# Gate and up of the later chunks with 76 products per tile pair instead of 78

## The chip, the cores and the metric

One core of a Trainium2 chip runs the whole program. The metric is the device time of one execution in microseconds; of several runs the median is taken. TensorE is written PE here, its weight loads PEld, VectorE DVE, ScalarE ACT, GpSimd POOL and SyncE, which issues the transfers, SP.

## What is computed

The reference normalizes 8192 tokens of 448 channels, mixes them with a spectral layer (a Fourier transform over the tokens, a small block MLP on each frequency, the inverse transform), adds the result to the input, normalizes again and adds a gated feed-forward layer:

```python
h = _layernorm(x) * (1 + ca) + sa
x = x + ga * _A_ref(h, A_w1, A_b1, A_w2, A_b2)           # rfft2, block MLP, shrink, irfft2
h = _layernorm(x) * (1 + cb) + sb
x = x + gb * ((_gelu(h @ w_gate) * (h @ w_up)) @ w_down)  # 448 -> 1792 -> 448
```

The change lies in the last line alone: the products `h @ w_gate` and `h @ w_up` of most tokens, and what prepares their operands.

## The kernel before

The spectral part fills the first 360 us. Then the tokens pass in 32 chunks of 256 (two blocks of 128). Every float32 operand of the feed-forward layer is held as two fp16 parts, hi and lo, and a product is the sum of hi by hi, hi by lo and lo by hi.

**Chunks 0 to 7** (`NSTD = 8`) compute gate and up in the plain way: `gate_up(i, k)` for k = 0 to 13 in the matmuls of line 1240, each followed by GELU (1276) and a multiplication (1281), by sums on GpSimd (`sums`, 1289 to 1292) and by a cut of the result into hi and lo (`quantize`, 1300 and 1301).

**Chunks 8 to 31** use a scheme in the manner of Strassen and Winograd. Channels and hidden units are split in two, the tokens of a chunk too, and seven products (A11, S1, S2, A12, S4, A22, S3, each with its own form of the weights and of the tokens) replace eight. A unit of work is one tile pair: 128 hidden units of each half, for gate and up (`pr` = 0 and 1). `mm(u, reg, f, x)` issues one of the seven; its list `terms` names the hi and lo parts, and each entry is one matmul for gate and one for up. 448 channels make 224 to a half, which is one tile of 128 rows and one of 96. The second tile is packed: the last 64 channels (384 to 448) are handled so that both halves of a tile's rows carry something. A11, S1 and S2 take five entries, the other four six, together 39 entries or 78 matmuls to a unit, in line 1483. Seven units (`NP = 7`) make a chunk, 24 chunks make 168 units.

A period of that stage issues `stage_a` of unit u, `stage_d` of u - 2, `stage_c` of u - 1 and `stage_b` of u on PE; between them stand ScalarE's copies of PSUM (`copy_b`, 1511, and `seed`, 1515), VectorE's sums (`joins`, 1520 and 1526), GELU (1532, 1540) and the multiplications (1536, 1543). Once a chunk the down projection of the chunk before runs between them (`phase`, `down`).

**Operands of the later chunks.** The token forms of chunk i + 1 or i + 2 are packed into the tile `pk` (25 tiles of 128 columns): ScalarE writes the hi parts (`wpack_hi`, line 1454), GpSimd the lo parts (`wpack_lo`, 1460), in five pieces k. Two such tiles alternate. SyncE transposes them in five transfers of five tiles into `nt` (`wtransposes`, 1466). The weight forms are made once, **during chunks 1 to 7**, for one tile t a chunk: `load_forms` loads raw weights `wr`, `form_sums` adds and subtracts their quarters a11, a12, a21, a22 on GpSimd (1673 to 1677), `forms_hi` and `forms_lo` cut each form n into hi on ScalarE (1707) and lo on VectorE (1712), and `store_forms` writes them to DRAM (1721). Form S2 = a21 + a22 - a11 has a tile of its own, `wf`.

**What sets the order.** Each engine works through its instructions in the order in which the code issues them. The tables `start` and `steady` name the place of each step of the preparation: a number is the index k of `gate_up` behind which it stands, and `m0`, `m1`, `m2` are three places inside `down`. In chunks 2 to 7 it is `steady` that holds. The splits of g and v for the inverse transform of a later chunk (`split_g`, `split_v`, line 117) are issued behind k = 1, the preparation of k = 2 after them.

`down(i, banks, mid)` runs seven products of 21 matmuls (lines 1313 to 1315). In chunks 0 to 7 it takes two banks of PSUM in turn for all products but the second. Its middle is

```python
S.copy(p1, product(i, heads[0][1], 0, rest))
V.tensor_tensor(o11, product(i, heads[1][1], 1, rest), p1, ALU.add)
mid(0)
S.copy(p4, product(i, banks(2), 2))
mid(1)
V.tensor_tensor(u2, product(i, banks(3), 4), p1, ALU.add)
V.tensor_tensor(u4, product(i, banks(4), 3), u2, ALU.add)
mid(2)
```

`S.copy(p1, ...)` is line 1340, `S.copy(p4, ...)` 1346, the sum u2 1349, the sum u4 1350. The product with `banks(4)` uses the bank that the copy p4 empties.

Of the kernel before, what the change touches and what calls it, by code (L numbers as in the profile page):

```python
# [10 lines left out]
F32 = mybir.dt.float32  # L11
F32R = mybir.dt.float32r
F16 = mybir.dt.float16
# [3 lines left out]
ALU = mybir.AluOpType  # L17

N = 8192
D = 448  # L20
# [4 lines left out]
CB = 2  # L25
# [10 lines left out]
PKW = 2 * D + 64  # L36
PKO = [0, 128, 256, 384, 448, 576, 704, 832]
NTT = len(PKO)
NXT = 25
LA = 2  # L40
NSTD = 8
WPARTS = ((0, 4), (4, 7))
# [8 lines left out]
def spectral_geglu(ctx, tc, x, w1, b1, w2, b2, wg, wu, wd, cvec, wmod, cf1, cs2, cmi, cgm, out):  # L51
    nc = tc.nc
    V, S, G, T = nc.vector, nc.scalar, nc.gpsimd, nc.tensor
# [90 lines left out]
    with ExitStack() as actx:  # L144
# [26 lines left out]
        q, y, t, nm, mu = (ap.tile([128, NB], F32, name=nm) for nm in ("q", "y", "t", "nm", "mu"))  # L171
# [201 lines left out]
        for g, bs in enumerate(groups):  # L373
            e = bs[-1]
# [34 lines left out]
    with ExitStack() as bctx:  # L409
# [225 lines left out]
        side = {}  # L635
# [87 lines left out]
        n = NB // 4  # L723
# [25 lines left out]
        raws = {}  # L749
# [208 lines left out]
        for n, i in enumerate([3, 4, 5, 5, 6, 7, 7, 8, 9, 10, 11, 12, 13, 14]):  # L958
            j, pr = divmod(n, 2)
# [26 lines left out]
        draws, nxt, x1t = {}, {}, {}  # L986

        x1s, x1n = [ep.tile([128, CB, D], F32, name="x10")], {}
# [6 lines left out]
        cp = None  # L995
# [96 lines left out]
    with ExitStack() as cctx:  # L1092
        cp = cctx.enter_context(tc.tile_pool(name="cp", bufs=1, side="right"))
        H = 128 * CB
        pkt = cp.tile([128, NXT * 128], F16, name="pk")
        wds = wds + [cp.tile([128, 2, 7, HC], F16, name=f"wd{t}") for t in range(len(wds), NP)]
        x1s += [cp.tile([128, CB, D], F32, name=f"x1{n}") for n in (1, 2)]
        pkts = [pkt]
        nts, acts, pgu, outs = {}, {}, {}, []

        def nt_tile():
# [330 lines left out]
        def pk_of(i):  # L1432
            return pkts[max(0, i - NSTD) % 2]

        def pieces(i, k):

            n, p = nxt[i]["n"], pk_of(i)
            if k == 0:
                return [(n[:, 0, 0:192], p[:, 0:192], [(128, 192, p[:, 192:256]), (0, 128, p[:, 256:384])])]
            if k in (1, 2):  # L1440
                o = (1152, 1664)[k - 1]
                return [(n[:, k - 1, 192:448], p[:, o : o + 256], [(0, 256, p[:, o + 256 : o + 512])])]
            if k == 3:
                p = p[:, 384:1152].rearrange("p (j c) -> p j c", j=2)
                src = nxt[i]["t"][:, 0:384].rearrange("p (j c) -> p j c", j=2)
                return [(src, p[:, :, 0:192], [(128, 192, p[:, :, 192:256]), (0, 128, p[:, :, 256:384])])]
            p = p[:, 2176:3200].rearrange("p (j c) -> p j c", j=2)
            src = nxt[i]["t"][:, 384:896].rearrange("p (j c) -> p j c", j=2)
            return [(src, p[:, :, 0:256], [(0, 256, p[:, :, 256:512])])]

        def wpack_hi(i, ks):
            for k in ks:
                for src, hi, _ in pieces(i, k):
                    S.copy(hi, src)

        def wpack_lo(i, ks, e=G):
            for k in ks:
                for src, hi, los in pieces(i, k):
                    for a, b, lo in los:
                        e.tensor_tensor(lo, src[..., a:b], hi[..., a:b], ALU.subtract)  # L1460

        def wtransposes(i, gs, w=5):
            if i not in nts:
                nts[i] = nt_tile()
            for g in gs:
                nc.sync.dma_start(
                    nts[i][:, w * g : w * g + w, :], pk_of(i)[:, 128 * w * g : 128 * w * (g + 1)], transpose=True
                )

        A11, S1, S2, A12, S4, A22, S3 = range(7)  # L1470
        B11, T1, T2, B21, B22, T3, T4 = 0, 3, 6, 9, 13, 17, 21
        RV, RY, RX = 0, 1, 2

        def mm(u, reg, f, x, start=False):

            ps2, slot, nt = sets[u % 3], wslot[slot_of[u]], nts[u // NP]
            if f in (A11, S1, S2):
                terms = [(0, f, x), (0, f, x + 2), (1, f, x), (0, 7 + f, x + 1), (1, 7 + f, x + 1)]
            else:
                terms = [(l, f + 7 * g, x + g + 2 * m) for g in range(2) for l, m in ((0, 0), (0, 1), (1, 0))]  # L1480
            for j, (hl, wt, xt) in enumerate(terms):
                for pr in range(2):
                    T.matmul(  # L1483
                        ps2[:, pr, reg * 128 : reg * 128 + 128],
                        slot[:, pr, hl, wt, :],
                        nt[:, xt, :],
                        start=start and j == 0,
                        stop=j == len(terms) - 1,
                        skip_group_check=True,
                    )  # L1490
# [175 lines left out]
        def form_sums(t, part):  # L1666
            r = raws[("w", t)]
            a11, a12, a21, a22 = (r[:, q, h : h + 3].rearrange("p c x -> p (c x)") for q in range(2) for h in (0, 3))
            if part == 0:
                raws[("f", t)] = cp2.tile([128, 384], F32, tag="wf", name="wf")  # L1670
            s2 = raws[("f", t)]
            if part == 0:
                G.tensor_tensor(a21, a21, a22, ALU.add)
                G.tensor_tensor(s2, a21, a11, ALU.subtract)
            else:
                G.tensor_tensor(a12, a12, s2, ALU.subtract)
                G.tensor_tensor(s2, a22, s2, ALU.subtract)

        def form_cut(t, n):

            w, r, s2 = raws[("s", t, n // 5)], raws[("w", t)], raws[("f", t)].rearrange("p (c x) -> p c x", c=3)
            tq = r[:, :, 6:7]
            f, c, src = [
                (A12, 0, r[:, 0, 3:6]),
                (A12, 3, tq[:, 0]),
                (A11, 0, r[:, 0, 0:3]),
                (S1, 0, r[:, 1, 0:3]),
                (S2, 0, s2),
                (A22, 0, r[:, 1, 3:6]),
                (S4, 3, tq[:, 0]),  # L1690
                (A22, 3, tq[:, 1].to_broadcast([128, 2, 128])),
                (S4, 0, r[:, 0, 3:6]),
                (S3, 0, s2),
            ][n]
            f0 = WPARTS[n // 5][0]

            def out(l):
                return w[:, l, 0:3, f - f0] if c == 0 else w[:, l, 3, f - f0 : f - f0 + src.shape[1]]

            return out(0), out(1), src  # L1700

        def forms_hi(t, *ns):
            for n in ns:
                if n % 5 == 0:
                    raws[("s", t, n // 5)] = cp2.tile([128, 2, 4, 4 - n // 5, 128], F16, tag=f"ws{n}", name="ws")
                hi, _, src = form_cut(t, n)
                S.activation(hi, src, AF.Copy, scale=sww)

        def forms_lo(t, *ns):
            for n in ns:  # L1710
                hi, lo, src = form_cut(t, n)
                V.scalar_tensor_tensor(lo, src, sww, hi, op0=ALU.mult, op1=ALU.subtract)
                if n == 4:
                    w = raws[("s", t, 0)]
                    V.tensor_copy(w[:, :, 3, 0:3], w[:, :, 2, 0:3])

        def store_forms(t, part):
            w = raws.pop(("s", t, part))
# [8 lines left out]
            ("m1", forms_lo, 0),  # L1727
            ("m1", forms_hi, 2),
            ("m2", forms_lo, 2),
            ("m2", forms_hi, 1, 3),  # L1730
            (3, forms_lo, 1, 3),
            (3, forms_hi, 4),
            (4, forms_lo, 4),
            (4, form_sums, 1),
            (4, forms_hi, 5),
            (5, forms_lo, 5),
            (5, forms_hi, 6, 7),
            (5, store_forms, 0),
            (6, forms_lo, 6, 7),
            (6, forms_hi, 8),  # L1740
            (7, forms_lo, 8),
            (7, forms_hi, 9),
            (8, forms_lo, 9),
            (9, store_forms, 1),
        ]
        steady = [
# [15 lines left out]
            (3, forms_lo, 6, 7),  # L1762
            (4, forms_hi, 8),
            (5, forms_lo, 8),
            (5, forms_hi, 9),
            (6, forms_lo, 9),
            (7, store_forms, 1),
        ]
        prep = {}
# [83 lines left out]
        pack_lo(0)  # L1853
        down_lo(0, range(1, 2))
        fctx.close()
        cp2 = cctx2.enter_context(tc.tile_pool(name="cp2", bufs=1))
        load_d8(2)
        load_g(1)
# [70 lines left out]
        pkts.append(cp2.tile([128, NXT * 128], F16, name="pk2"))  # L1929
        x1s.append(cp2.tile([128, CB, D], F32, name="x13"))  # L1930

        opening = {
# [13 lines left out]
        for u in range(U0, NT_ + 1):  # L1946
            period(u)
            i, k = divmod(u, NP)
# [99 lines left out]
```

## Time and profile before

| | us |
|---|---|
| median of three runs | 1865.55 |
| lowest and highest | 1863.15, 1866.06 |
| the profiled execution | 1862.79 |
| its span, first to last instruction | 1861.0 |
| line 1483: 13104 matmuls, in union | 736.5 |
| lines 1313 to 1315 into `pdn`: each 1218 matmuls, in union | 315 to 316 |
| line 1240: 2464 matmuls, in union | 268.3 |

A group's time is the union of its instructions, and matmuls overlap (each lasts longer than the distance to the next), so the groups' times don't add up to PE's. A row of the timeline gives the start, the length, the engine, the line, the operation, output and input, and in brackets how long the engine stood idle before it and what ended that.

### The profile page before, as it was taken

To read this page: it belongs to the slowest core of one execution; us is meant where nothing else is said; L and a number is where in the kernel's file an instruction comes from. 1 tells how busy PE (TensorE), PEld (TensorE's weight loads), DVE (VectorE), ACT (ScalarE), POOL (GpSimd) and SP (SyncE) were. 2 spreads that over 40 slices of the span, in tenths; PEclk is the share of its full clock that TensorE was granted. 3 is DMA by queue.
4 is the path that set the end of the run, shared out by engine and by line. 5 is a ranking of instruction groups with operands and counts; after the bars stand their busy time and mean duration, and the time that the engine had idled before them with its cause. 6 is when DMAs were issued, how large, how long until landed. Compare 5 with 4: busy or idle time off the path is not lost.

```text
span 1861.0 us, 56443 instructions
## 1 busy us (share of the span) xinstructions
PE 1821.3 (98%) x23376; PEld 1726.6 (93%) x23376; DVE 1410.8 (76%) x2895; ACT 973.6 (52%) x1828; POOL 1313.2 (71%) x1705
## 2 busy tenths in 40 slices
PE   7999999899999999999999999999999999999998
PEld 3698999788888899999999999999999999999998
DVE  8787999878766677777777777777777777777755
ACT  5776778544444444555555555555554444444443
POOL 3476878258777778777777777777777777777544
PEclk9999999999999999999999999999999999999999
DMA  9987778744444446966766666666666676666551
GB/s 355 337 288 250 234 202 230 206 106 104 105 104 104 104 105 171 248 170 171 171 176 177 174 176 172 171 172 174 178 173 178 173 175 175 174 176 174 154 158 55
DMA packets 380089, 330.48 MB, mean 178 GB/s; under 512 B 110260, under 2 KB 358200, under 8 KB 379832
## 3 DMA queue, kind: packets, MB, share of 16 engines
q1 hardware_dynamic: 379832, 326.87, 64.0%
q8 instruction: 183, 3.00, 0.7%
q14 instruction: 74, 0.61, 0.1%
HBM read 243.32 MB, written 60.10 MB: 163 GB/s over the span
## 4 chain that ended last, share of the span: by engine, by line
PE 86%; DVE 6%; DMA 3%; ACT 2%; SPq 1%; POOL 1%; issue 1%; ACTq 0%; DVEq 0%
PE set L1483 39%; PE pgu L1240 11%; PE pdn L1313 6%; PE pdn L1315 6%; PE pdn L1314 6%; PE ps L213 2%; PE set L1315 2%; PE set L1314 2%; PE set L1313 2%; DVE y L556 1%; DVE hl L486 1%; PE set L1607 1%; PE pm L539 1%; PE ps L451 1%; DVE st L174 1%
## 5 line engine op out<-in xcount | busy, mean ns | idle before, releaser
L1483 PE MATMUL set<-nt,wk 128*128 128x128 f16 x13104 | 736.5, 219 | 3.1 <-ACT sb L1511 1.6
L1483 PEld LDWEIGHTS <-wk 128*128 128x128 f16 x13104 | 733.9, 98 | 3.5 <-issue 2.4
L1315 PE MATMUL pdn<-wd,ac 128*128 128x224 f16 x1218 | 315.5, 259 | 0.6 <-DVE ac L1301 0.6
L1313 PE MATMUL pdn<-wd,ac 128*128 128x224 f16 x1218 | 315.7, 259 | 0.0
L1314 PE MATMUL pdn<-wd,ac 128*128 128x224 f16 x1218 | 315.5, 259 | 0.0
L1240 PE MATMUL pgu<-nt,wk 128*128 128x256 f16 (+1 forms) x2464 | 268.3, 273 | 3.8 <-DVE x L1281 3.8
L1240 PEld LDWEIGHTS <-wk 128*128 128x128 f16 (+1 forms) x2464 | 225.8, 98 | 44.9 <-issue 19.3
L1532 ACT ACTIVATE gl<-c,dg 128x384 f32<-128x384 f32 x168 | 103.5, 616 | 229.9 <-DVE c L1526 227.0
L1558 DVE SCALAR_TENSOR_TENSOR ac<-x,sa_act,ac 128x896 f16<-128x896 f32 x168 | 205.9, 1226 | 19.9 <-ACT ac L1548 19.8
L1289 POOL TENSOR_TENSOR x<-x 128x128 f32<-128x128 f32 x223 | 129.8, 582 | 119.9 <-DVE x L1281 58.5
L1359 POOL TENSOR_TENSOR cq<-cq 128x224 f32<-128x224 f32 x32 | 21.1, 660 | 261.8 <-DVE cq L1358 261.8
L1290 POOL TENSOR_TENSOR x<-x 128x128 f32<-128x128 f32 x223 | 186.3, 836 | 17.5
L1548 ACT ACTIVATE ac<-x,sa_act 128x896 f16<-128x896 f32 x168 | 174.2, 1037 | 13.8 <-POOL x L1292 6.6
L1536 DVE TENSOR_TENSOR x<-c,gl 128x384 f32<-128x384 f32 x168 | 154.3, 918 | 17.3 <-ACT gl L1532 17.0
L1313 PEld LDWEIGHTS <-ac 128*128 128x128 f16 x1568 | 153.4, 98 | 4.9 <-issue 4.8
L1315 PEld LDWEIGHTS <-ac 128*128 128x128 f16 x1568 | 153.4, 98 | 0.8 <-DVE ac L1301 0.8
L1314 PEld LDWEIGHTS <-ac 128*128 128x128 f16 x1568 | 153.5, 98 | 0.1
L1520 DVE TENSOR_TENSOR c<-set,sb 128x512 f32<-128x512 f32 x168 | 115.3, 687 | 35.6 <-PE set L1483 35.6
L1276 ACT ACTIVATE gel<-pgu,dg 128x256 f32<-128x256 f32 x112 | 49.5, 471 | 157.9 <-PE pgu L1240 150.3
L1291 POOL TENSOR_TENSOR x<-x 128x128 f32<-128x128 f32 x223 | 131.8, 591 | 0.0
L1511 ACT COPY sb<-set 128x512 f32<-128x512 f32 x168 | 97.6, 581 | 62.0 <-PE set L1483 60.7
L117 POOL TENSOR_TENSOR yl<-y,yh 128x448 fp32r<-128x448 f32 x63 | 87.9, 1413 | 54.9 <-ACT yh L115 54.6
(334 smaller groups left out, 3837.1 us busy)
## 6 DMA issues: line engine op xcount, KB each, us to landing
wk<-wk SPq DMA_DIRECT2D x76, 1024.0 KB, 8.9
wk<-wk SPq DMA_DIRECT2D x76, 768.0 KB, 5.7
tr<-td SPq DMA_DIRECT2D x32, 448.0 KB, 4.9
vd<-us SPq DMA_DIRECT2D x64, 224.0 KB, 3.1
xx<-in_A_x SPq DMA_DIRECT2D x32, 448.0 KB, 4.5
v<-vd SPq DMA_DIRECT2D x63, 224.0 KB, 5.5
out<-x SPq DMA_DIRECT2D x31, 448.0 KB, 7.0
xt<-in_A_x SPq DMA_DIRECT2D x15, 896.0 KB, 14.7
```

Source lines behind the costliest of these rows:

```text
L1240: T.matmul(pgu[i, t, q][:, pr * H : (pr + 1) * H], ws[rows, n, w, tw], nts[i][rows, tn, :], start=start, stop=stop, skip_group_check=True,)
L1289: e.tensor_tensor(s1, a21, a22, ALU.add)
L1290: e.tensor_tensor(s2, s1, a11, ALU.subtract)
L1291: e.tensor_tensor(s3, a11, a21, ALU.subtract)
L1313: T.matmul(ps, ac[:, 0, ka], w[:, 0, kb], start=n == 0, stop=False)
L1314: T.matmul(ps, ac[:, 0, ka], w[:, 1, kb], start=False, stop=False)
L1315: T.matmul(ps, ac[:, 1, ka], w[:, 0, kb], start=False, stop=n == NP - 1)
L1483: T.matmul(ps2[:, pr, reg * 128 : reg * 128 + 128], slot[:, pr, hl, wt, :], nt[:, xt, :], start=start and j == 0, stop=j == len(terms) - 1 ...
L1520: V.tensor_tensor(c[:, :, 1:3, :], p[:, :, 0:256].rearrange("p g (r c) -> p g r c", r=2), b[:, :, 0:128].rearrange("p g (o c) -> p g o c", ...
L1536: V.tensor_tensor(xs[u][:, 1::3, :], cts.pop(u)[:, 1], gls.pop(u), ALU.mult)
L1548: S.activation(ac[:, 0], xs[u][:, 0:7], AF.Copy, scale=sa_act[:, t : t + 1])
L1558: V.scalar_tensor_tensor(ac[:, 1], xs.pop(u)[:, 0:7], sa_act[:, t : t + 1], ac[:, 0], op0=ALU.mult, op1=ALU.subtract)
```

## The change

It takes one of the six entries from S4, which makes 76 matmuls to a unit, and lets half-used tiles of A11, S2 and S4 carry the terms of the last 64 channels. For that,

- the weight forms hold other things in their packed halves: `form_sums` makes a difference of the last 64 channels' weights (`e1`), form 7 of before goes, form S3 gets a packed column of its own, and small copies and one addition (`forms_lo`, `forms_hi`) fill the halves;
- `form_sums` has three parts instead of two, and the tile `wf` goes: S2 overwrites a11, which it may do once `forms_hi` and `forms_lo` of form 2 (A11) have read a11. So it moves from place 0 to place 2 in `steady`;
- the packed tokens have 27 tiles instead of 25: 7 in `pkx`, of which there are two, and 20 in `pk`, of which there is one. The first transpose takes seven tiles, the other four take five;
- one of the buffers for x moves to another pool.

The core of the diff:

```diff
 def wpack_hi(i, ks):
+    n = nxt[i]["n"]
     for k in ks:
         for src, hi, _ in pieces(i, k):
             S.copy(hi, src)
+        if k == 2:
+            for src, o in ((n[:, 1, 320:384], 1152), (n[:, 0, 128:192], 1280), (n[:, 1, 384:448], 2496)):
+                S.copy(pkt[:, o : o + 64], src)
+        if k == 3:
+            S.copy(pkt[:, 2432:2496], nxt[i]["t"][:, 320:384])
...
+            if k == 2:
...
+                e.tensor_tensor(rest, a, b, ALU.subtract)
+                el = pkx_of(i)[:, 832:896]
+                e.tensor_tensor(el, el, rest[:, 1], ALU.subtract)
...
-    if f in (A11, S1, S2):
-        terms = [(0, f, x), (0, f, x + 2), (1, f, x), (0, 7 + f, x + 1), (1, 7 + f, x + 1)]
+    if f in (A11, S1, S2, S4):
+        x4, x5 = {A11: (x + 1, TA), S1: (x + 1, x + 1), S2: (x + 1, TY), S4: (x + 3, x + 1)}[f]
+        terms = [(0, f, x), (0, f, x + 2), (1, f, x), (0, 7 + f, x4), (1, 7 + f, x5)]
...
 def form_sums(t, part):
...
     if part == 0:
         G.tensor_tensor(a21, a21, a22, ALU.add)
-        G.tensor_tensor(s2, a21, a11, ALU.subtract)
+    elif part == 1:
+        G.tensor_tensor(a11, a21, a11, ALU.subtract)
     else:
-        G.tensor_tensor(a12, a12, s2, ALU.subtract)
-        G.tensor_tensor(s2, a22, s2, ALU.subtract)
+        e1, e2 = r[:, 0, 6], r[:, 1, 6]
+        G.tensor_tensor(e1, e2, e1, ALU.subtract)
+        G.tensor_tensor(a12, a12, a11, ALU.subtract)
+        G.tensor_tensor(a11, a22, a11, ALU.subtract)
...
 steady = [
...
     (2, forms_lo, 2),
+    (2, form_sums, 1),
     (2, forms_hi, 1),
     ("m0", forms_lo, 1),
     ("m0", forms_hi, 3, 4),
...
     ("m2", forms_lo, 4, 5),
-    ("m2", form_sums, 1),
-    ("m2", forms_hi, 6, 7),
+    ("m2", form_sums, 2),
+    ("m2", forms_hi, 6),
```

How the instructions stand on GpSimd in chunk 2, at the second `gate_up` and the down projection (`x` are the sums, `gl` and `v` the splits, `wr` the quarters of the weights, `wf` S2; 1359 belongs to the down projection). Before:

```order
L1673 TENSOR_TENSOR wr<-wr 128x384
L1674 TENSOR_TENSOR wf<-wr 128x384
L1289 TENSOR_TENSOR x_7216<-x_7216 128x128
L1290 TENSOR_TENSOR x_7216<-x_7216 128x128
L1291 TENSOR_TENSOR x_7216<-x_7216 128x128
L1292 TENSOR_TENSOR x_7216<-x_7216 128x128
L117 TENSOR_TENSOR gl<-g,gh 128x256
L117 TENSOR_TENSOR v<-v,vh 128x896
L1676 TENSOR_TENSOR wr<-wr,wf 128x384
L1677 TENSOR_TENSOR wf<-wr,wf 128x384
L1359 TENSOR_TENSOR cq_3433<-cq_3432 128x224
```

With the change:

```order
L1683 TENSOR_TENSOR wr<-wr 128x384
L1289 TENSOR_TENSOR x_7221<-x_7221 128x128
L1290 TENSOR_TENSOR x_7221<-x_7221 128x128
L1291 TENSOR_TENSOR x_7221<-x_7221 128x128
L1292 TENSOR_TENSOR x_7221<-x_7221 128x128
L117 TENSOR_TENSOR gl<-g,gh 128x256
L117 TENSOR_TENSOR v<-v,vh 128x896
L1685 TENSOR_TENSOR wr<-wr 128x384
L1688 TENSOR_TENSOR wr<-wr 128x128
L1689 TENSOR_TENSOR wr<-wr 128x384
L1690 TENSOR_TENSOR wr<-wr 128x384
L1359 TENSOR_TENSOR cq_3433<-cq_3432 128x224
```

S2 (1674 before, 1685 now) moved from ahead of the four sums and the two splits to behind them.

ScalarE in the down projection of the same chunk (1340 is the copy p1, 1346 the copy p4, the two rows between them are the hi parts of forms S1 and S2). Before:

```order
L1707 ACTIVATE ws<-wr,sww 128x128
L1340 COPY cq_3432<-pdn 128x224
L1707 ACTIVATE ws<-wr,sww 128x3x128
L1707 ACTIVATE ws<-wf,sww 128x3x128
L1346 COPY cq_3432<-pdn 128x224
```

With the change:

```order
L1719 ACTIVATE ws<-wr,sww 128x128
L1340 COPY cq_3432<-pdn 128x224
L1719 ACTIVATE ws<-wr,sww 128x3x128 x2
L1346 COPY cq_3432<-pdn 128x224
L1719 ACTIVATE ws<-wr,sww 128x3x128
```

Nothing moved here: the hi part of S2 stands ahead of the copy p4 in both, and reads `wf` before and `wr` (a11) now.

GpSimd in chunk 7, where the tokens of chunk 8 are packed as well. Before:

```order
L1426 COPY x_10642<-n_10542 128x64
L1460 TENSOR_TENSOR pk<-n_10542,pk 128x64
L1460 TENSOR_TENSOR pk<-n_10542,pk 128x128
L1460 TENSOR_TENSOR pk<-n_10542,pk 128x256 x2
L1289 TENSOR_TENSOR x_10635<-x_10635 128x128
```

With the change:

```order
L1426 COPY x_10662<-n_10564 128x64
L1467 TENSOR_TENSOR pkx_5786<-n_10564,pkx_5786 128x64
L1467 TENSOR_TENSOR pkx_5786<-n_10564,pkx_5786 128x128
L1467 TENSOR_TENSOR pkx_5786<-n_10564,pkx_5786 128x256
L1467 TENSOR_TENSOR pk<-n_10564,pk 128x128
L1471 TENSOR_TENSOR pk<-n_10564,pk 128x2x64
L1473 TENSOR_TENSOR pkx_5786<-pkx_5786,pk 128x64
L1289 TENSOR_TENSOR x_10657<-x_10657 128x128
```

One subtraction of 256 columns became one of 128, one of two times 64 and one of 64.

More of the change, by code (lines that the diff above doesn't have):

```diff
@@ L38 @@
 NTT = len(PKO)
-NXT = 25
+NXT, NXP = 27, 7
 LA = 2
@@ L1094, in spectral_geglu @@
         H = 128 * CB
-        pkt = cp.tile([128, NXT * 128], F16, name="pk")
+        pkt = cp.tile([128, (NXT - NXP) * 128], F16, name="pk")
+        pkx = [cp.tile([128, NXP * 128], F16, name="pkx0")]
         wds = wds + [cp.tile([128, 2, 7, HC], F16, name=f"wd{t}") for t in range(len(wds), NP)]
-        x1s += [cp.tile([128, CB, D], F32, name=f"x1{n}") for n in (1, 2)]
-        pkts = [pkt]
+        x1s.append(cp.tile([128, CB, D], F32, name="x11"))
         nts, acts, pgu, outs = {}, {}, {}, []
@@ L1460, in wpack_lo, with wtransposes @@
                         e.tensor_tensor(lo, src[..., a:b], hi[..., a:b], ALU.subtract)
-        def wtransposes(i, gs, w=5):
+                    if k == 2:
+                        rest = pkt[:, 1152:1408].rearrange("p (j c) -> p j c", j=2)[:, :, 64:128]
+                        a, b = (v[:, 128:256].rearrange("p (j c) -> p j c", j=2) for v in (src, hi))
+                        e.tensor_tensor(rest, a, b, ALU.subtract)
+                        el = pkx_of(i)[:, 832:896]
+                        e.tensor_tensor(el, el, rest[:, 1], ALU.subtract)
+        def wtransposes(i, gs):
             if i not in nts:
@@ L1465, in wtransposes @@
             for g in gs:
[L1466 to L1471, printed above, removed]
+                t, w, src = (0, NXP, pkx_of(i)) if g == 0 else (NXP + 5 * g - 5, 5, pkt[:, 640 * g - 640 : 640 * g])
+                nc.sync.dma_start(nts[i][:, t : t + w, :], src, transpose=True)
+        A11, S1, S2, A12, S4, S3, A22 = range(7)
+        B11, B21, T1, T2, B22, TA, T3, T4, TY = 0, 3, 7, 10, 13, 17, 18, 22, 26
         RV, RY, RX = 0, 1, 2
@@ L1707, in forms_hi @@
                 S.activation(hi, src, AF.Copy, scale=sww)
+                if n == 7:
+                    w = raws[("s", t, 1)]
+                    S.copy(w[:, 0, 3, 0], w[:, 0, 2, 0])
         def forms_lo(t, *ns):
@@ L1712, in forms_lo @@
                 V.scalar_tensor_tensor(lo, src, sww, hi, op0=ALU.mult, op1=ALU.subtract)
-                if n == 4:
-                    w = raws[("s", t, 0)]
-                    V.tensor_copy(w[:, :, 3, 0:3], w[:, :, 2, 0:3])
+                w, e = raws[("s", t, n // 5)], raws[("s", t, 0)][:, :, 3, 3]
+                if n == 1:
+                    V.tensor_copy(w[:, 1, 3, 0:3:2], e[:, 0:1].to_broadcast([128, 2, 128]))
+                elif n == 4:
+                    V.tensor_copy(w[:, 0, 3, 0:3], w[:, 0, 2, 0:3])
+                    V.tensor_copy(w[:, 1, 3, 1], w[:, 1, 2, 1])
+                elif n == 5:
+                    V.tensor_copy(w[:, 1, 3, 0], e[:, 1])
+                elif n == 6:
+                    V.tensor_tensor(w[:, 1, 3, 1], w[:, 1, 3, 1], w[:, 1, 3, 0], ALU.add)
         def store_forms(t, part):
-            w = raws.pop(("s", t, part))
+            w = raws[("s", t, part)]
             for pr, rows in enumerate(rows2):
@@ L1733, in spectral_geglu @@
             (4, forms_lo, 4),
-            (4, form_sums, 1),
+            (4, form_sums, 2),
             (4, forms_hi, 5),
             (5, forms_lo, 5),
-            (5, forms_hi, 6, 7),
+            (5, forms_hi, 6),
             (5, store_forms, 0),
[L1739 to L1743, printed above, removed]
+            (6, forms_lo, 6),
+            (6, forms_hi, 7),
+            (7, forms_lo, 7),
+            (7, forms_hi, 8),
+            (8, forms_lo, 8),
             (9, store_forms, 1),
@@ L1758, in spectral_geglu @@
             ("m2", forms_lo, 4, 5),
-            ("m2", form_sums, 1),
-            ("m2", forms_hi, 6, 7),
+            ("m2", form_sums, 2),
+            ("m2", forms_hi, 6),
             (3, store_forms, 0),
[L1762 to L1766, printed above, removed]
+            (3, forms_lo, 6),
+            (4, forms_hi, 7),
+            (5, forms_lo, 7),
+            (5, forms_hi, 8),
+            (6, forms_lo, 8),
             (7, store_forms, 1),
@@ L1855, in spectral_geglu @@
         fctx.close()
+        cpx = cctx.enter_context(tc.tile_pool(name="cpx", bufs=1, side="right"))
+        x1s.append(cpx.tile([128, CB, D], F32, name="x12"))
         cp2 = cctx2.enter_context(tc.tile_pool(name="cp2", bufs=1))
@@ L1928, in spectral_geglu @@
         sets = [sets[(n - U0) % 3] for n in range(3)]
-        pkts.append(cp2.tile([128, NXT * 128], F16, name="pk2"))
+        pkx.append(cp2.tile([128, NXP * 128], F16, name="pkx1"))
         x1s.append(cp2.tile([128, CB, D], F32, name="x13"))
```

33 lines of the change are left out of this document (15 added, 18 removed).

## Prediction

> **What bounds the kernel now.** I read the head of the page first, then the busy time by stage, then TensorE's own waits, then the chain that ended last.
>
> ```profile
> span 1861.0 us, 56443 instructions
> PE 1821.3 (98%) x23376; PEld 1726.6 (93%) x23376; DVE 1410.8 (76%) x2895; ACT 973.6 (52%) x1828; POOL 1313.2 (71%) x1705
> ```
> ```profile
> 360.00:740.00 380.00, 375.66 (x3543) 332.69 (x3542) 272.87 (x510) 162.39 (x287) 278.15 (x337) 1.00 0.50 116
> 760.00:1100.00 340.00, 340.00 (x5168) 338.04 (x5167) 257.68 (x522) 169.59 (x324) 252.99 (x351) 1.00 0.68 177
> ```
> The columns are the stretch, its length, and the busy us of PE, PEld, DVE, ACT and POOL, then the granted clock. Chunks 0 to 7 run from about 360 to 740, and there PE is busy 375.66 of 380 us. The later chunks, 8 to 31, begin at 740, and there it is busy throughout. These are the waits of PE in the two stretches (from 740 on; then from 360 to 740):
>
> ```profile
> PE set L1483 <- ACT sb L1511: 1.6, 1, 1.6
> PE set L1483 <- DMA wk<-wk: 1.0, 1, 1.0
> PE set L1483 <- DVE c L1526: 0.6, 1, 0.6
> ...
> PE pgu L1240 <- DVE x L1281: 3.8, 6, 1.1
> ```
> So both stages are bound by PE, in which a matmul less is worth its spacing, and a wait more costs its length. No later slack takes either back.
>
> **What is removed.** Each of the 168 tile pairs of the later chunks loses one product of two halves, that is two matmuls with their weight loads: 336 of 13104.
>
> ```profile
> 814.86 30.48 PE set L1483 x546
> 860.73 30.48 PE set L1483 x546
> ```
> In the chain these rows are one chunk's 546 matmuls: 30.48 / 546 = 55.8 ns each, and 336 x 55.8 ns = 18.8 us. The first pair's share falls before the two waits at the opening of this stage and is lost, so I take **18.7 us off**.
>
> **What the later chunks get in exchange.** Per chunk, ScalarE makes four more 64-column copies, GpSimd two more small subtractions, and the first transpose has 7 tiles where it had 5. The fullest period is the one that carries three of the copies; in the chunk at 1181 it reads:
>
> ```profile
> 1190.88 0.41 ACT L1454 CAST pk<-n 128x256 f16<-128x256 f32 x1
> 1192.35 0.59 ACT L1511 COPY sb<-set 128x512 f32<-128x512 f32 x1 [0.54 <-PE set L1483]
> 1193.48 0.29 DVE L1543 TENSOR_TENSOR x<-set,gl 128x128 f32<-128x128 f32 x1 [0.49 <-ACT gl L1540]
> 1167.44 9.23 SPq L1466 DMA_TRANSPOSE nt<-pk x4
> ```
> A 64-column copy isn't in the trace: it costs between nothing and the 0.41 of 256 columns. I take 0.25, a little nearer the row, so 0.75 for three. ScalarE waits 0.54 us for PE behind them, and the copy sb (L1511) that follows is due only two stages later. VectorE behind it still has 0.49 to spare. I cost them at nothing; without this cover they would be 0.2 us in each of 23 chunks. The single buffer pk adds a wait of ScalarE's cast for the transposes of the chunk before: those were issued by 1176.67, 14 us ahead of the cast at 1190.88. That is nothing either, up to 14 us of landing.
>
> **What the change puts in the way in chunks 2 to 7.** There the weight forms for the later chunks are prepared between the products of the down projection, one tile a chunk. Before, form S2 was made in a buffer of its own, right after the first addition. Now it overwrites a11, so GpSimd may make it only once a11 has been cut into both halves, and it stands behind the splits of g and v. This is GpSimd in chunk 3:
>
> ```profile
> 507.17 1.85 POOL L1673 TENSOR_TENSOR wr<-wr 128x384 f32<-128x384 f32 x1
> 509.10 1.19 POOL L1674 TENSOR_TENSOR wf<-wr 128x384 f32<-128x384 f32 x1
> 510.25 0.78 POOL L1289 TENSOR_TENSOR x<-x 128x128 f32<-128x128 f32 x1
> ...
> 512.27 0.45 POOL L1292 TENSOR_TENSOR x<-x 128x128 f32<-128x128 f32 x1
> 512.68 0.73 POOL L117 TENSOR_TENSOR gl<-g,gh 128x256 fp32r<-128x256 f32 x1
> 513.37 2.08 POOL L117 TENSOR_TENSOR v<-v,vh 128x896 fp32r<-128x896 f32 x1
> 515.40 1.00 POOL L1676 TENSOR_TENSOR wr<-wr,wf 128x384 f32<-128x384 f32 x1
> ```
> ScalarE cuts S2 to fp16 (`L1707 ws<-wf`) *ahead of* its copy p4 (`L1346`), which empties the bank of the third product. That copy is what lets PE begin the product after the next, in the same bank:
>
> ```profile
> 510.85 0.60 ACT L1707 ACTIVATE ws<-wf,sww 128x384 f16<-128x384 f32 x1
> 512.39 0.35 ACT L1346 COPY cq<-pdn 128x224 f32<-128x224 f32 x1 [0.94 <-PE pdn L1315]
> ...
> 514.40 0.39 DVE L1349 TENSOR_TENSOR cq<-pdn,cq 128x224 f32<-128x224 f32 x1 [2.41 <-PE pdn L1315]
> ```
> That the cut waits for GpSimd's S2 shows in chunk 2, where it starts as `L1674` ends (462.82 + 1.19 = 464.01):
>
> ```profile
> 464.05 0.61 ACT L1707 ACTIVATE ws<-wf,sww 128x384 f16<-128x384 f32 x1 [0.30 <-POOL wf L1674]
> ```
> Worked for chunk 3: the split of v ended at 515.45. Without `L1674` and the 0.08 us ahead of it this is 514.18. S2 then takes the 1.00 of `L1676`, of the same shape at the same place: 515.2. The cut takes 0.60, and the copy behind it 0.35 less a small overlap: the bank is free at 516.1. PE finishes the product in between as `L1349` starts, and would have gone on at about 514.3. It stands 1.8 us. The four sums move under VectorE's work before 511 (0.78 against 0.45 in the rows), for which I add 0.2: **2.0 us**. Chunks 4, 5 and 6 have the same rows in the same order, and I take 2.0 for each. Chunks 2 and 7:
>
> ```profile
> 462.82 1.19 POOL L1674 TENSOR_TENSOR wf<-wr 128x384 f32<-128x384 f32 x1
> ...
> 467.10 2.07 POOL L117 TENSOR_TENSOR v<-v,vh 128x896 fp32r<-128x896 f32 x1
> ...
> 466.56 0.39 DVE L1349 TENSOR_TENSOR cq<-pdn,cq 128x224 f32<-128x224 f32 x1 [0.84 <-PE pdn L1315]
> ...
> 699.11 1.00 POOL L1674 TENSOR_TENSOR wf<-wr 128x384 f32<-128x384 f32 x1
> ...
> 701.11 2.60 POOL L1460 TENSOR_TENSOR pk<-n,pk 128x64 f16<-128x64 f32 x4
> ...
> 708.57 2.08 POOL L117 TENSOR_TENSOR v<-v,vh 128x896 fp32r<-128x896 f32 x1
> 707.07 0.39 DVE L1349 TENSOR_TENSOR cq<-pdn,cq 128x224 f32<-128x224 f32 x1 [2.00 <-PE pdn L1315]
> ```
> Chunk 2: v ends at 469.17, less 1.27 is 467.9; 1.95 for S2, cut and copy gives 469.85. PE would have gone on at 466.45. With the same 0.2: 3.6 us. Chunk 7 also packs chunk 8, and six small subtractions stand where four took 2.60; I put 0.65 more (one more of their mean; the two are small). 710.65 - 1.08 + 0.65 = 710.2, and 712.15 with the 1.95. PE would have gone on at 706.95: 5.2, and 5.4 with the 0.2. Sum of the stalls: 3.6 + 4 x 2.0 + 5.4 = **17.0 us**. Bounds: if the four sums ran at 0.45 each, 0.7 less in each of six, 12.8; if S2 took the 1.85 of `L1673`, 0.85 more in each, 22.1.
>
> **What a stall does to the clock.** In the profile the granted clock moves on a grid of 3.41 us. I cut the span at its edges:
>
> ```profile
> 99.50:102.91 3.41, 1.52 (x17) 1.01 (x15) 3.24 (x7) 1.73 (x5) 2.00 (x2) 1.00 0.19 70
> 102.91:106.33 3.42, 3.40 (x18) 2.94 (x19) 2.92 (x6) 1.94 (x4) 3.02 (x3) 0.50 0.61 153
> ...
> 239.45:242.86 3.41, 1.78 (x18) 1.28 (x15) 3.32 (x7) 2.07 (x5) 1.88 (x3) 1.00 0.02 4
> 242.86:246.27 3.41, 3.41 (x20) 3.12 (x18) 3.33 (x9) 2.49 (x4) 3.33 (x3) 0.50 0.78 191
> 744.56:747.97 3.41, 1.94 (x34) 1.88 (x33) 1.54 (x4) 3.41 (x5) 2.51 (x5) 1.00 1.09 347
> 747.97:751.39 3.42, 2.46 (x45) 2.35 (x43) 2.84 (x4) 3.20 (x10) 3.42 (x6) 1.00 1.11 338
> ```
> A slice in which PE was busy 1.52 or 1.78 us was followed by one at half clock, a slice with 1.94 was not. So about 1.55 us of idleness inside one slice costs half of the next, 1.7 us of matmuls. A stall of 2.0 shows as some 1.8 of idle; it lies on the grid so that one slice holds 1.55 of it with a chance of (3.41 - 1.55 + 0.25) / 3.41 = 0.6. Four such chunks: 2.4 halvings, 4.1 us. Chunks 2 and 7 always halve; part of the halved slice may lie in the stall itself, so 1.4 and 1.5. Together **7.0 us**, between nothing and eight halvings (13.6).
>
> The Trainium skill, "TensorE: Matmul & The Clock Gate", Part 1, has PE drop to half clock after at least one idle window of some 3.4 us, on a grid that runs free, and warns only of gaps longer than that. By it the 2.0 us stalls would not halve the clock; this trace has halvings after shorter gaps, and I go by the trace. The grid's length agrees with the page.
>
> **Small terms.** In chunk 1 the forms are cut along VectorE's part of the path (the six waits for `L1281`, 3.8 us, all end before 455). The copies there change from one to several:
>
> ```profile
> L1715 DVE COPY ws<-ws 128x768 f16<-128x768 f16 x7 | 4.5, 650 | 0.2
> ```
> Four narrower copies and an addition stand where one of 0.65 us and one cut stood: between nothing and two such rows, 1.3; I take 0.5. At the opening of the later chunks SyncE's queue is full, and the wider transpose may push it: 0.3, between 0 and 1.
>
> **Sum.** The profiled execution took 1862.79 us (its span of 1861.0 and 1.8 around it): 1862.79 - 18.7 + 17.0 + 7.0 + 0.5 + 0.3 = 1868.9, **6.1 us more**. The median of the runs, 1865.55, is 2.8 above that execution, so on its scale I forecast 1871.6. A measurement here can tell 0.2%, 3.7 us, from no change.
>
> **Rivals.** *The stalls come, the clock holds.* If only a slice that is idle for all its 3.41 us halved the next, chunks 3 to 6 would pay nothing, and without any halving 7.0 goes: 1864.6 to 1867.6. The Trainium skill's page cited above would have it so. The slice of 239.45 speaks against it. *GpSimd is early enough.* Then PE never waits for p4 and the removed matmuls arrive whole: 1865.55 - 18.7 + 0.8 = 1847.7, **faster**. It is decided at S2 in chunks 2 to 7: GpSimd would have to reach it 2.0 us sooner in chunks 3 to 6, 3.6 and 5.4 in 2 and 7. For it speaks that spans on POOL are rough; against it that its rows from 507.17 to 516.4 follow one another without a gap. *Everything at its upper bound*, or a wait in the later chunks that I cost at nothing: 22.1 + 10 of halvings, 1880. That fewer matmuls are issued than stated is no rival: the difference of the two instruction streams on PE is 336 loads and 336 matmuls, nothing else.
>
> **Numbers.** Stalls and halvings as worked out 0.60, with a range of its own of 1866 to 1878; the clock holds 0.17; GpSimd early 0.11; upper bounds 0.12. The range of 1861 to 1880 leaves out the faster rival and most of the last. Slower by over 0.2% (above 1869.3): some 0.45 of the first case and the last, 0.57. Faster: 0.12. Within: 0.31.
>
> **What would show it.** L1483's successor with x12768 and a chain of 532 matmuls of 29.7 us a chunk: the saving. PE's wait `pdn <- ACT cq` six times, 17 us in total, longest in chunk 7, with ScalarE's cut of S2 waiting for POOL just ahead: the stalls. Slices at clock 0.5 between 465 and 730: the halvings. I am wrong if PE shows no wait for ScalarE in chunks 2 to 7, or if the later chunks have waits of PE that repeat every chunk.

## The result and the profile after

| | before | with the change |
|---|---|---|
| median, us (four runs each) | 1864.52 | 1879.93 |
| lowest and highest | 1863.15, 1866.06 | 1875.86, 1880.26 |
| ratio, 95% interval | | 1.0077 (1.006 to 1.0095) |
| the profiled execution | 1862.79 | 1880.26 |
| its span | 1861.0 | 1878.5 |

The change makes the kernel 0.8% slower, 15.4 us by the medians. The forecast was 1871.6 in a range of 1861 to 1880: the sign was right, the time lies 0.07 us inside the end of the range, and the loss is 2.5 times the 6.1 us that the sum gave. So the sum left out some 9 us, more than its whole forecast.

The page of the changed kernel, its head, the chain that ended last by engine, and the group of the thinned matmuls:

```profile
span 1878.5 us, 55991 instructions
...
PE 41%; POOL 35%; DVE 9%; issue 6%; DMA 5%; ACT 2%; SPq 1%; POOLq 0%; ACTq 0%; DVEq 0%
...
L1496 PE MATMUL set<-nt,wk 128*128 128x128 f16 x12768 | 717.8, 219 | 2.4 <-DMA wk<-wk 1.1
```

The matmuls went as stated, 12768 of them (line 1496 is 1483 of before). But the chain now runs through GpSimd for 35% of the span. GpSimd is busy only 71% of the span; it is in the chain because of *when* it finishes something.

The two stages are split by where the first and the last of a line's matmuls start. These are the rows for line 1240 (chunks 0 to 7) and for the thinned matmuls, first before, then with the change:

```profile
L1240 PE MATMUL pgu<-nt,wk x2464: 266/273/421, 359.7 to 740.0; 128*128 128x256 f16 x173, 64*128 64x256 f16 x17
L1483 PE MATMUL set<-nt,wk x13104: 216/219/230, 740.1 to 1844.3; 128*128 128x128 f16 x199
```
```profile
L1240 PE MATMUL pgu<-nt,wk x2464: 266/273/421, 363.0 to 768.7; 128*128 128x256 f16 x173, 64*128 64x256 f16 x17
L1496 PE MATMUL set<-nt,wk x12768: 216/219/230, 768.8 to 1861.8; 128*128 128x128 f16 x200
```

Between the two profiled executions that makes three differences. Up to the first matmul of chunk 0: 3.3 us. From there to the later chunks: 405.8 against 380.4 us, **25.4 more** (forecast 24.5: stalls, clock and chunk 1). From there to the end of the span: 1109.7 against 1120.9, **11.2 less** (forecast 18.4 less). The first is not the change's: in the profiles of the experiments below, none of which alters that part, the same matmul starts anywhere from 358.7 to 363.9. The last is where the forecast failed.

PE's waits from 360 to 740, then the weight loads' own waits in the later chunks from 816 to 1850:

```profile
PE pdn L1313 <- ACT cq L1346: 17.0, 6, 5.1
PE pgu L1240 <- DVE x L1281: 4.6, 7, 1.2
...
PEld set L1621 <- POOL gl L117: 8.7, 21, 0.4
```

The first row is the forecast stall, six times, 17.0 us. The third is new and was in no part of the forecast: the load of the weights for line 1621 waits for the split of g on GpSimd (`gl`, line 117) in 21 chunks of the window, 0.4 us each. It doesn't appear among the waits of PE's matmuls, because it is the load that carries the semaphore. Line 1621 belongs to `winverse`, the inverse transform of a coming chunk, which stands just ahead of the down projection.

The place in one chunk, GpSimd and the weight loads, with the change:

```profile
917.15 0.72 POOL L117 TENSOR_TENSOR gl<-g,gh 128x256 fp32r<-128x256 f32 x1
...
932.16 0.66 POOL L1359 TENSOR_TENSOR cq<-cq 128x224 f32<-128x224 f32 x1 [9.39 <-DVE cq L1358]
...
917.33 0.19 PEld L1620 LDWEIGHTS set<-vh,gh 128*128 128x128 f32 x1
917.93 0.19 PEld L1621 LDWEIGHTS set<-vh,gl 128*128 128x128 f32 x1 [0.40 <-POOL gl L117]
```

and the same place before (1608 is what 1621 is now):

```profile
889.85 0.72 POOL L117 TENSOR_TENSOR gl<-g,gh 128x256 fp32r<-128x256 f32 x1
...
905.45 0.66 POOL L1359 TENSOR_TENSOR cq<-cq 128x224 f32<-128x224 f32 x1 [9.97 <-DVE cq L1358]
...
891.11 0.19 PEld L1608 LDWEIGHTS set<-vh,gl 128*128 128x128 f32 x1
```

Before, the split ended at 890.57 and the load came at 891.11: **0.54 us to spare**, which is all the cover that a chunk had. A saving of 14 matmuls takes 0.78 us out of PE's chunk (30.48 against 29.70 in the chain). GpSimd's work between the down projection (1359) and the next split of g takes a little longer than before: 889.85 + 45.87 - 905.45 = 30.27 us before, 917.15 + 45.47 - 932.16 = 30.46 now. 0.54 - 0.78 - 0.19 = -0.43, and the wait measures 0.40. A chunk takes 45.47 us now (the mean of the 21 distances between the first matmuls of chunks 9 to 30, 45.45 to 45.50) against 45.87, so only 0.40 of the 0.78 arrives.

The stall in chunk 2, on GpSimd and ScalarE:

```profile
469.41 1.04 POOL L117 TENSOR_TENSOR gl<-g,gh 128x256 fp32r<-128x256 f32 x1
470.42 2.07 POOL L117 TENSOR_TENSOR v<-v,vh 128x896 fp32r<-128x896 f32 x1
472.44 0.99 POOL L1685 TENSOR_TENSOR wr<-wr 128x384 f32<-128x384 f32 x1
...
473.47 0.61 ACT L1719 ACTIVATE ws<-wr,sww 128x384 f16<-128x384 f32 x1 [5.57 <-POOL wr L1685]
473.99 0.33 ACT L1346 COPY cq<-pdn 128x224 f32<-128x224 f32 x1
```

GpSimd's rows follow one another, S2 (1685) comes last, ScalarE stands 5.57 us in front of its cut of S2, and the copy p4 (1346) goes out only behind it.

### The profile page after: what moved, and what is told of

Same layout as the page of the kernel before. It is cut to its first block, busy times and chain, and to the rows that moved or that the text cites. A ratio compares the mean times of both kernels' runs of the same rounds, so it can differ in the third digit from the quotient of the medians.

```text
span 1878.5 us, 55991 instructions
## 1 busy us (share of the span) xinstructions
PE 1818.6 (97%) x23040; PEld 1713.3 (91%) x23040; DVE 1395.4 (74%) x2916; ACT 994.9 (53%) x1924; POOL 1330.9 (71%) x1760
## 4 chain that ended last, share of the span: by engine, by line
PE 41%; POOL 35%; DVE 9%; issue 6%; DMA 5%; ACT 2%; SPq 1%; POOLq 0%; ACTq 0%; DVEq 0%
POOL x L1290 6%; PE pdn L1313 5%; PE pdn L1315 5%; PE pdn L1314 5%; PE set L1496 4%; POOL x L1289 4%; PE pgu L1240 4%; POOL x L1292 4%; POOL pk L1467 3%; POOL v L1123 3%; POOL x L1328 3%; POOL cq L1327 3%; PE set L1313 2%; PE set L1315 2%; PE set L1314 2%
## 5 line engine op out<-in xcount | busy, mean ns | idle before, releaser
L1496 PE MATMUL set<-nt,wk 128*128 128x128 f16 x12768 | 717.8, 219 | 2.4 <-DMA wk<-wk 1.1
L1496 PEld LDWEIGHTS <-wk 128*128 128x128 f16 x12768 | 715.2, 98 | 2.9 <-issue 1.5
L1313 PE MATMUL pdn<-wd,ac 128*128 128x224 f16 x1218 | 318.9, 262 | 17.0 <-ACT cq L1346 17.0
L1315 PE MATMUL pdn<-wd,ac 128*128 128x224 f16 x1218 | 318.7, 262 | 0.6 <-DVE ac L1301 0.6
L1314 PE MATMUL pdn<-wd,ac 128*128 128x224 f16 x1218 | 318.7, 262 | 0.0
L1571 DVE SCALAR_TENSOR_TENSOR ac<-x,sa_act,ac 128x896 f16<-128x896 f32 x168 | 213.5, 1271 | 38.1 <-ACT ac L1561 38.1
L1289 POOL TENSOR_TENSOR x<-x 128x128 f32<-128x128 f32 x223 | 146.5, 657 | 109.2 <-DVE x L1281 61.0
L1290 POOL TENSOR_TENSOR x<-x 128x128 f32<-128x128 f32 x223 | 193.1, 866 | 17.5
L1561 ACT ACTIVATE ac<-x,sa_act 128x896 f16<-128x896 f32 x168 | 174.8, 1040 | 48.8 <-POOL x L1292 42.0
L1291 POOL TENSOR_TENSOR x<-x 128x128 f32<-128x128 f32 x223 | 166.9, 748 | 0.0
L1549 DVE TENSOR_TENSOR x<-c,gl 128x384 f32<-128x384 f32 x168 | 142.9, 851 | 18.1 <-ACT gl L1545 17.1
L556 DVE SCALAR_TENSOR_TENSOR y<-pm,lam,t 64x224 f32<-64x224 f32 x256 | 115.1, 449 | 10.5 <-ACT t L548 6.7
```

Source lines behind the costliest of these rows:

```text
L1289: e.tensor_tensor(s1, a21, a22, ALU.add)
L1290: e.tensor_tensor(s2, s1, a11, ALU.subtract)
L1291: e.tensor_tensor(s3, a11, a21, ALU.subtract)
L1313: T.matmul(ps, ac[:, 0, ka], w[:, 0, kb], start=n == 0, stop=False)
L1314: T.matmul(ps, ac[:, 0, ka], w[:, 1, kb], start=False, stop=False)
L1315: T.matmul(ps, ac[:, 1, ka], w[:, 0, kb], start=False, stop=n == NP - 1)
```

## The experiments

All ratios are against the kernel before, run on the same chip. The changed kernel is compared by its 1879.93 us from the result; the kernel before took 1864.52 us there and 1865.55 and 1864.67 beside the experiments, so such differences are good to about 1 us.

### The cut of S2 behind the copy p4

```diff
-            ("m0", forms_hi, 3, 4),
+            ("m0", forms_hi, 3),
...
-            ("m1", forms_hi, 5),
+            ("m1", forms_hi, 4, 5),
```

> The changed kernel with one step moved: ScalarE's cut of S2 in chunks 2 to 7 stands behind the copy p4 instead of ahead of it; GpSimd's order is as in the changed kernel. My theory: the six waits of PE for the copy p4 (17.0 us) go, and with them the four halved slices of the clock (some 1.7 us each): 1879.9 - 17.0 - 6.8 = 1856, and no wait of PE for ScalarE's cq. The later chunks still take 45.47 us each. Rival (the wait only changes its place): the late S2 also holds VectorE's cut, which stands ahead of the sum that empties the bank of the last product; then PE waits there for VectorE about as long, and the time stays within 5 us of 1880.

1857.04 us, ratio 0.996 (0.9946 to 0.9973): 22.9 us less than the changed kernel. PE's waits from 360 to 740:

```profile
PE pgu L1240 <- DVE x L1281: 4.6, 7, 1.2
PE ptr L1222 <- ACT pk L1195: 3.6, 2, 2.7
PE ptr L1222 <- ACT nt L1233: 0.9, 2, 0.7
PE pdn L1315 <- DVE ac L1301: 0.6, 1, 0.6
```

No wait for the copy p4 is left, and none for VectorE has come in its place; the rival falls. (The two `ptr` rows belong to the start of chunk 0, and are there before the change too, ahead of 360.) Chunks 0 to 7 take from 363.9 to 745.7, 381.8 us, 24.0 less than with the change: 17.0 of stall, and 7.0 that I put down to the clock. A later chunk stays at 45.49. The opening got longer: from the first matmul of chunk 8 to that of chunk 9 it takes 51.7 us, against 47.4 with the change.

### The split of g one period earlier

```diff
-            0: [(2, split_v)],
-            1: [(2, split_g), (1, wtransposes, [0])],
+            0: [(2, split_g), (2, split_v)],
+            1: [(1, wtransposes, [0])],
```

> The changed kernel with one step moved: in the later chunks GpSimd splits g one period earlier, ahead of the split of v; nothing else changes. My theory: the 0.42 us a chunk in which PE's weight load waits for the split of g go; split of v now ends last on GpSimd, over 2 us before it is needed. A chunk takes 45.09 us instead of 45.47; 22 chunks, 8.4 us: 1879.9 - 8.4 = 1871.5. Rival (GpSimd's work is too much wherever it stands, or the wider transposes and the copies cost the time): a chunk stays at 45.4 to 45.5 and the time within 2 us of 1880.

1871.52 us, ratio 1.0032 (1.0021 to 1.0044): 8.4 us less, as expected. The six waits for p4 are all there (17.1 us). GpSimd in one chunk, and the chain's matmuls in two:

```profile
996.30 0.73 POOL L117 TENSOR_TENSOR gl<-g,gh 128x256 fp32r<-128x256 f32 x1
996.99 3.75 POOL L1123 TENSOR_TENSOR v<-v,vh 128x224 fp32r<-128x224 f32 x4
```
```profile
1107.53 29.70 PE set L1496 x532
1152.60 27.41 PE set L1496 x491
```

1152.60 - 1107.53 = 45.07 us a chunk, which is 45.87 less the whole 0.78 to within 0.02. So the wider transposes and the additional copies on ScalarE cost nothing, as was forecast, and the rival falls.

### Less work on GpSimd

In `wpack_lo`, the lo parts of 64 channels and their correction (lines 1471 and 1473, 0.54 and 0.30 us) are left out for the tokens of chunks 10 to 31:

```diff
-                    if k == 2:
+                    if k == 2 and i <= NSTD + 1:
                         rest = pkt[:, 1152:1408].rearrange("p (j c) -> p j c", j=2)[:, :, 64:128]
```

> The changed kernel in which, for the tokens of chunks 10 to 31, GpSimd leaves out the two small subtractions that the change added (lines 1471 and 1473: the lo parts of 64 channels and their correction); the splits stay where they are. My theory has two parts in the 0.42 us: PE's chunk is 0.78 us shorter while GpSimd's chain from the down projection to the split of g is 0.18 longer, and before it had some 0.55 to spare. Without the 0.84 us of the two subtractions the chain is early again: a chunk of 45.09 to 45.2 us, no wait for gl, 1879.9 - 8 = 1872. Rival (VectorE's products, which the sums wait for, set the chain, not GpSimd's own work): the sums wait instead, half of the wait or more stays, 45.3 to 45.47 a chunk, 1876 to 1880.

1869.13 us, ratio 1.0022 (1.0012 to 1.0032), 3 us under the 1872 expected, which is no more than runs of one kernel differ here. There is no wait for gl. The chain's matmuls, and GpSimd in one chunk:

```profile
1109.44 29.70 PE set L1496 x532
1154.52 25.52 PE set L1496 x457
```
```profile
912.68 0.73 POOL L117 TENSOR_TENSOR gl<-g,gh 128x256 fp32r<-128x256 f32 x1
...
927.95 0.66 POOL L1359 TENSOR_TENSOR cq<-cq 128x224 f32<-128x224 f32 x1 [9.64 <-DVE cq L1358]
```

A chunk takes 45.08 us. GpSimd's chain from 1359 to the next split of g became 912.68 + 45.09 - 927.95 = 29.82 us, 0.64 less for 0.84 of work removed. So the chain is mostly GpSimd's own work, and moving the split or thinning the chain ahead of it does the same.

### Both moves

> The changed kernel with both moves. My theory has the two losses independent: 1879.9 - 23.8 - 8.4 = 1847.7, which is 18 us less than the kernel before, that is the whole price of the 336 matmuls. Rival (the losses share a cause or uncover a third): it stays over 1853.

1849.51 us, ratio 0.9917 (0.9903 to 0.9931): faster than both kernels, 15 to 16 us below the one before. PE's waits from 740 on:

```profile
PE set L1496 <- ACT sb L1524: 2.7, 1, 2.7
PE set L1496 <- DVE n L1190: 1.2, 1, 1.2
PE set L1496 <- DMA wk<-wk: 1.1, 1, 1.1
PE set L1496 <- DVE c L1539: 0.6, 1, 0.6
```

Each comes once: the first three at the opening of the later chunks, the last at the end. The losses are nearly independent (22.9 and 8.4 apart, 30.4 together). At the opening 50.7 us pass from the first matmul of chunk 8 to that of chunk 9, against 48.8 before and 47.4 with the change, so part of the removed stall comes back there. ScalarE waits there for the load of v:

```profile
747.97 0.94 ACT L1120 CAST vh<-v 128x896 fp32r<-128x896 f32 x1 [4.42 <-DMA v<-vd]
```

With the change this wait was 1.0 us, before 1.9. All four kernels with the stall in chunk 7 take 47.4 to 48.1 us here, the five without it 48.8 to 51.7. That the stall gives SyncE time to issue the load fits this, but no run shows it alone.

### S2 late in the kernel before

```diff
             if part == 0:
                 raws[("f", t)] = cp2.tile([128, 384], F32, tag="wf", name="wf")
...
                 G.tensor_tensor(a21, a21, a22, ALU.add)
+                if t == 0:
+                    G.tensor_tensor(s2, a21, a11, ALU.subtract)
+            elif part == 2:
                 G.tensor_tensor(s2, a21, a11, ALU.subtract)
...
             (2, forms_lo, 2),
+            (2, form_sums, 2),
             (2, forms_hi, 1),
```

> The kernel before, with all its 78 products, in which only the subtraction that makes S2 in chunks 2 to 7 is issued at the place that it has in the changed kernel (behind k = 2, so on GpSimd behind the splits of g and v); its buffer of its own stays. My theory: the place alone makes the stall: six waits of PE for the copy p4 of 16 to 17 us together, and three to five halved slices: 1864.5 + 16.5 + 6.8 = 1888. Rival (the stall needs the other new work, small copies and the addition): under 10 us of waits, below 1876.

1886.65 us, ratio 1.0109 (1.0089 to 1.0129): the one subtraction, issued later, costs 21 us with all 78 products in place. PE's waits from 360 on:

```profile
PE pdn L1313 <- ACT cq L1346: 16.4, 6, 4.5
PE pgu L1240 <- DVE x L1281: 4.2, 6, 1.1
```

The place on GpSimd alone makes the stall, 16.4 us against 17.0. The rest of the new work has at most the 0.6 between them, which lies in chunk 7 (4.51 us against 5.06).

### S2 early, with the cut where it was

Early split of g as above, and

```diff
-            (0, forms_hi, 0),
-            (1, forms_lo, 0),
-            (1, forms_hi, 2),
-            (2, forms_lo, 2),
-            (2, form_sums, 1),
+            (0, forms_hi, 0, 2),
+            (1, forms_lo, 2),
+            (1, form_sums, 1),
+            (2, forms_lo, 0),
```

> The changed kernel with the early split of g, and with S2 made earlier in chunks 2 to 7: a11 is cut into both halves behind k = 0 and 1, and GpSimd's subtraction is issued behind k = 1, ahead of the splits of g and v; ScalarE's cut of S2 stays ahead of the copy p4. My theory (what matters is when GpSimd has S2, not where the cut stands): no wait of PE for the copy p4, and since all forms are cut and stored earlier than with the cut behind p4, SyncE reaches the load of v sooner at the opening of the later chunks, where 50.7 us pass in the first chunk with both moves: some 2 us less there, 1847.5. Rival one: a11's lo half at k = 1 holds up VectorE, PE waits for L1281 once or twice a chunk, 1 us each, and the time is 1853 or more. Rival two (SyncE's queue at the opening is full with or without earlier forms): 1849.5 as with both moves.

1848.91 us, ratio 0.9911 (0.9893 to 0.9929). PE's waits from 360 to 742:

```profile
PE pgu L1240 <- DVE x L1281: 5.3, 7, 1.4
PE pdn L1315 <- DVE ac L1301: 1.2, 1, 1.2
PE pdn L1313 <- ACT cq L1346: 0.2, 1, 0.2
```

With S2 ahead of the splits the cut may stand where it stood, so it is the time of S2 that counts. PE's waits for VectorE come to 6.5 us here against 5.2 with the cut behind p4, 1.3 more in all and not per chunk, so the first rival falls. The opening still takes 50.1 us: my expectation of 2 us less fell, and the time is that of the second rival. ScalarE still waits 3.2 us there for the load of v. The two versions can't be told apart (1849.5 and 1848.9).

### A control: both moves in the kernel before

The two diffs of the first two experiments, applied to the kernel before.

> The kernel before with the same two moves (the cut of S2 behind the copy p4; the split of g one period earlier), as a control. My theory: before the change neither wait existed, so the moves gain nothing: 45.87 us a chunk and 1865.5, within 2 us. Rival (the moves are gains of their own, and the kernel with both moves is faster for that reason and not for its fewer matmuls): 1860 or less.

1866.37 us, ratio 1.0002 (0.9991 to 1.0012), and 45.87 us a chunk (1139.72 - 1093.86 in the chain):

```profile
1093.86 30.48 PE set L1483 x546
1139.72 30.48 PE set L1483 x546
```

The moves gain nothing of their own. What the versions with both gain is the matmuls'.

## Why the prediction was right, and where it was wrong

**The saving.** 336 matmuls at 55.8 ns, 18.7 us: right as PE's own work, where the chain has 29.70 us for 532 matmuls. In the changed kernel only 11.2 of it arrived. With both losses gone the kernel is 15 to 16 us faster than before, most of the rest of the 18.7 going at the opening of the later chunks.

**The stall.** Forecast 3.6, four times 2.0, and 5.4, together 17.0; the gaps of PE measured 3.69, 1.99, 2.15, 1.98, 2.14 and 5.06, together 17.0. The mechanism (S2 behind the splits, the cut ahead of the copy p4, the bank) is shown by the late S2 in the kernel before, which makes it, and by the moved cut and the early S2, which remove it. The forecast could be this close because it took rows of GpSimd that follow one another without a gap, and shifted them. That the sums agree to the tenth is luck: the forecast was 0.35 us too low for chunks 2 to 6 and 0.34 too high for chunk 7.

**The clock.** Forecast 7.0 us, with 2.4 halved slices in chunks 3 to 6. Measured 7.0 us as the rest of the 24.0 that the moved cut took back, with halved slices behind the stalls of chunks 2, 4, 6 and 7. That rest holds whatever else differs between the two profiles; four halved slices of 3.41 us cost at most 6.8. So the size is right, and the same tenth is luck. Two slices of chunks 3 and 4 with what came behind each:

```profile
522.31:525.72 3.41, 1.71 (x18) 1.55 (x17) 0.39 (x1) 0.61 (x2) 3.41 (x4) 1.00 0.00 0
525.72:529.14 3.42, 3.14 (x33) 3.13 (x33) 0.93 (x3) 1.15 (x3) 0.72 (x1) 1.00 0.00 0
573.51:576.92 3.41, 1.26 (x14) 1.10 (x13) 1.81 (x2) 1.01 (x3) 3.41 (x4) 1.00 0.02 5
576.92:580.33 3.41, 3.41 (x20) 2.79 (x19) 0.00 (x0) 0.74 (x2) 0.32 (x1) 0.50 0.00 0
```

1.70 us of idleness in a slice let the clock be, 2.15 halved the next. The bound of 1.55 that I took from the stage before 360 was too low here; it made the chance for a halving 0.6, and over the 16 stalls of about 2 us in the four kernels that have them it was 7 of 16. That moved the sum by less than 2 us. The rule that I weighed, of the Trainium skill's "TensorE: Matmul & The Clock Gate", Part 1, at least one whole idle window of some 3.4 us before the clock drops, does not hold in these traces: the slice at 573.51 was idle for 2.15 of 3.41 us. The time that it would have given, 1864.6 to 1867.6, did not come. The prediction's words that the page warns only of longer gaps went too far: the same Part, under "A second HAM failure mode", tells of a kernel whose frequent short idle stretches made the clock swing.

**What the later chunks get in exchange: the step that failed.** I costed it at nothing, with the words that ScalarE has 0.54 us and VectorE 0.49 to spare. For these two engines that was right: a copy of 64 columns took 0.245 us, and with the split of g out of the way a chunk takes the 45.08 us that the saving alone gives. GpSimd, the engine that the change gives the other small subtractions, was left out of that check, and so was a plainer thing: *the saving itself* uses up slack. The premise that in a stage where PE is busy throughout "a matmul less is worth its spacing" failed here. Every chain that runs beside PE once a chunk has to fit into a chunk that is 0.78 us shorter. The row of before that would have told, the split of g ending 0.54 us ahead of the load of line 1608, is not among PE's waits, because there was none yet. Cost: 0.39 us in each of 21 chunks, 8.3 us by the profiles with the late and the early split (the expectation counted 22), 8.4 by the medians. Of 0.97 us by which the slack fell, the shorter chunk makes 0.78 and the longer chain 0.19; the early split and the thinner GpSimd chain each undo it.

The prediction named waits of PE that repeat every chunk as a sign of being wrong, and they came, on the weight loads. So the first case, with its own range of 1866 to 1878, did not come as worked out; what came is its stalls and halvings and, on top, "a wait in the later chunks that I cost at nothing", which stood in the last case at 0.12. That the time still lies inside the outer range, by 0.07 us, is luck.

**Small terms.** Chunk 1: the waits for `L1281` went from 3.8 to 4.6 us, 0.8 against 0.5 forecast. The opening: forecast 0.3 more; it took 47.4 us against 48.8, 0.6 less than the removed products explain, probably because the stall in chunk 7 gave SyncE time. Without the stall the changed kernel takes 50.1 to 51.7, but the control, whose products are the old ones, takes 50.5 too; so most of it is not the change's. The cut behind p4 alone, the early S2 and the control also have a halved slice there. What in SyncE's queue makes the late load, the runs don't settle.

**The sum.** Forecast 6.1 us more on the profiled execution; measured 17.5. The difference of 11.4 is 8.3 of the split of g and 3.3 of the start, which differs between executions of any of these kernels; the small terms take out one another. By the medians the loss is 15.4, since the profiled execution of before lay under its four runs and that of the change was the slowest of its four.

## What to carry to other kernels

When matmuls are taken out of a loop that PE fills, list every chain that another engine runs once a turn, and compare its spare time ahead of PE's use (end of the producer against the start of the load or matmul that needs it) with the time saved a turn: slack that no wait shows yet is spent first. When a buffer is shared to save space and a step moves behind others for it, look at what stands in order behind its *reader*: here one subtraction of 1 us cost 17 us and 7 of clock, through a copy that had nothing to do with it. And look at such a stall before giving a change up: two steps moved in the tables of places turned 15 us of loss into 15 us of gain.

## What the runs showed of the hardware

From the first matmul of line 1240 on, nine profiles agree on when the clock halves. PE's idleness is taken here as the profile models it. Of all slices of the 3.41 us grid between 365 and 1830 us, the 20 in which PE was idle for 1.98 us or more (up to 3.41) were each followed by a slice at 0.5, and the 53 with 0.9 to 1.75 us of idleness were not once. So somewhere between 51 and 58% of a slice lies the bound for this mix of matmuls. In the spectral stage of before a slice with 1.78 us of busy PE, idle for 1.63, was followed by a halved one, so this bound is not that of the whole kernel. In the later stages a stall of 2.0 us therefore costs 2.0 us or, with half of the next 3.41, 3.7, by where it falls on the grid: of 16 such stalls 7 were followed by a halved slice. Two executions of one kernel can then differ by such steps. Four runs of the changed kernel span 4.4 us, the fastest at a mean granted clock of 0.992 and the others at 0.988 to 0.990; that the clock makes the whole of that spread is not shown.
